# Building the constant mask-edge tile on GpSimd behind the first gate/up blocks

## The chip, the cores and the metric

The kernel runs on one core of a Trainium2 chip. The metric is the device time of one execution in microseconds. A core has five engines that run side by side, each through its own in-order stream of instructions: TensorE (PE, matmuls; its weight loads are shown as PEld), VectorE (DVE), ScalarE (ACT), GpSimd (POOL) and SyncE (SP, which issues most of the DMAs here). They wait for one another by semaphores.

## What is computed

One normalised input goes through two branches whose sums are added to it: a causal sliding-window attention (32 heads of 20, window 256) and a gated MLP.

```python
xn = layernorm(x)                         # x: 1 x 2048 x 640, bf16
q, k, v = split(xn @ wqkv)                # 32 heads of 20
scores = q @ k.T * 20 ** -0.5
mask = (i - j >= 0) & (i - j < 256)       # query i, key j
o = softmax(where(mask, scores, -1e9)) @ v
A = o @ wo
h = sigmoid(xn @ w_gate) * (xn @ w_up)    # 2048 x 1536
B = h @ w_down
return x + A + B
```

## The kernel before, in words

The 2048 rows are worked in four chunks of 512 (c = 0 to 3). For each chunk the kernel normalises x, projects q, k and v, runs the gate and up projections in twelve blocks of 128 hidden units, computes scores and p times v, and at the end multiplies with w_down and wo and adds x.

Scores are made in steps. A step of the function scores fills one PSUM tile ps with scores of four heads for two groups, laid in units of 64 keys by 64 queries (matmuls at L487); ScalarE takes the exponential into a bf16 tile pT (L493); then the units that the mask cuts through are trimmed. In most steps GpSimd does this with four affine selects (L504): two of 64 x 512 elements for the diagonal units of either half of the partitions, and two of 64 x 256 for the oldest units. In steps with the key "late" (one of five per head pair from the second chunk on) the trimming is one VectorE instruction, a minimum with the constant tile edge (L497), which is 128 x 512, zero where the mask forbids and a huge number elsewhere. The steps of the first chunk, the table FIRST, have no "late".

Edge is built by make_edge (L238): one memset (L239) and four affine selects of 64 x 256 (L243), all on GpSimd. It is called at L675, when the code has already emitted the first chunk's norms and projections. GpSimd has no part in those beyond constants and memsets, so in its own stream edge follows directly on the memsets of the v tiles (L320, L321) and precedes the first select.

The function pv (L508) multiplies the pT tiles of one head pair with v (L520). In the first chunk it reads four score tiles in nine pieces; each piece is a set of eight small matmuls, and a matmul waits for those selects of its tile that it reads. The last piece belongs to the fourth tile.

The order of the work from L677 on is written by a small planner. fill is a list of parts, each a generator with a cost in nanoseconds of TensorE. Between the score steps the main loop (L719) pulls matmul work out of the parts in order, as much as a budget allows; the first pull (L715) takes six half gate/up blocks ahead of the first score step. A part made by later() runs its function once, at cost 0, when the parts in front of it are used up. The first part, gu0a, holds gate/up blocks 0 to 3 of the first chunk, with the statistics of the second chunk's norm mixed in between. The reciprocal roots of those norms are two GpSimd instructions (rstds, L266 and L267); from them VectorE makes the normalised rows xn (L272), which SyncE's queue transposes by DMA into xnT (L283). The order of each engine's stream is the order in which this code emits instructions; nothing reorders them afterwards.

Of the kernel before, what the change touches and what calls it, by code (L numbers as in the profile page):

```python
# [93 lines left out]
def kernel(  # L94
# [95 lines left out]
    def load_rest():  # L190
        load_gu(wg, B_w_gate, 1, 0, FS // 2)
        load_gu(wu, B_w_up, 1, 0, FS // 2)
        load_gu(wg, B_w_gate, 1, FS // 2)
        load_gu(wu, B_w_up, 1, FS // 2)
        spread("q", 0, 4, NG)
        spread("k", 0, 4, NG)
# [39 lines left out]
    edge = const.tile([P, HG, 2 * U], BF16, name="edge")  # L236

    def make_edge():  # L238
        nc.gpsimd.memset(edge, BIG)  # L239
        for k, base, sign in ((0, -1, -1), (1, 0, 1)):  # L240
            for a in range(2):
                view = edge[a * U:(a + 1) * U, :, k * U:(k + 1) * U]
                nc.gpsimd.affine_select(out=view, in_=view, pattern=[[0, HG], [sign, U]],  # L243
                                        compare_op=GE, fill=0.0, base=base, channel_multiplier=-sign)
# [98 lines left out]
    def g_norms(c, turn, gap=3):  # L343


        new_xnT(c)
        mvs = lnp.tile([P, SBC, nc.vector.BN_AGGR_DIM], FP32, name="mvs", bufs=1)
        for s in range(SBC):
            ln_block(c, s, mvs[:, s, :])
            if s == SBC - 1:  # L350
                rstds = rstd_blocks(mvs)
            yield 0
        for _ in range(gap):
            yield 0
        for s in range(SBC):
            norm_block(c, s, mvs[:, s, :], rstds[:, s:s + 1])
            yield 0
            if turn:
                turn_block(c, s)
# [43 lines left out]
    def part(w, d, f):  # L403
        k, first = divmod(f * P, FS)
        return w[k][:, d, first:first + P]

    def g_gu(c, f0, f1):
        for f in range(f0, f1):
            pg = ps_d.tile([P, CW], FP32, name="pg", tag="d")
            for d in range(DC):  # L410
                nc.tensor.matmul(pg, lhsT=part(wg, d, f), rhs=xnT[c][:, d, :],  # L411
                                 start=(d == 0), stop=(d == DC - 1))
            th = tp.tile([P, CW], FP32, name="th")
            nc.scalar.activation(out=th, in_=pg, func=TANH, scale=0.5)  # L414
            yield 5 * MM
            pu = ps_d.tile([P, CW], FP32, name="pu", tag="d")
            for d in range(DC):
                nc.tensor.matmul(pu, lhsT=part(wu, d, f), rhs=xnT[c][:, d, :],  # L418
                                 start=(d == 0), stop=(d == DC - 1))
            h = hp.tile([P, CW], BF16, name="h")  # L420
            ht[c, f] = h
            nc.vector.scalar_tensor_tensor(out=h, in0=th, scalar=1.0, in1=pu, op0=ADD, op1=MULT)  # L422
            yield 5 * MM
# [171 lines left out]
    def mix(a, b, first, every=1, rest=True):  # L595

        for k, cost in enumerate(a):
            yield cost
            if k >= first and (k - first) % every == 0:
                yield next(b, 0)  # L600
        if rest:
            yield from b
# [69 lines left out]
    for _ in g_qk(0):  # L672
        pass
    load_rest()
    make_edge()  # L675

    fill = Fill()  # L677
    GU = 10 * MM
# [3 lines left out]
    def later(load, *args):  # L682
        load(*args)
        yield 0
# [2 lines left out]
    norms2 = g_norms(2, True)  # L687
    norms3 = g_norms(3, False, 6)
    fill.add("gu0a", mix(g_gu(0, 0, 4), norms1, 4, 1, False), 4 * GU)
    fill.add("gu0b", mix(g_gu(0, 4, 12), norms1, 0), 8 * GU)  # L690
    fill.add("x2", later(load_x, 2), 0)
    fill.add("wo_i", later(turn_wo), 0)
# [114 lines left out]
```

## Time and profile before

| what | value |
|---|---|
| time, median of three runs | 309.31 us (308.95 to 309.39) |
| span of the profiled execution | 307.5 us |
| granted TensorE clock | 1.000 over the span |
| busy: TensorE, ScalarE, VectorE, GpSimd | 299.6, 198.4, 170.7, 169.3 us |
| edge: memset and four selects on GpSimd | 0.69 us at 3.18, and 1.79 us from 3.94 |
| first mask select on GpSimd (L504) | 32.70 us |
| first use of edge (L497) | 94.2 us |

The profile is of one execution; its span runs from the first to the last instruction. The time of a run is a little longer than the span; the profile gives no time of its own for the profiled execution besides the span, and the three runs' median lies 1.8 us above it. In the rows that follow, a line of the time order has the start, the duration, the engine, the source line, the operation and its tiles, and in brackets the idle time before it with what ended it. Several equal instructions behind one another are merged into one row (x4). The chain of work that ended last is followed back from the last instruction, at each step to what released it.

### The profile page before, as it was taken

Reading aid. Unit: us, or ns where it says so; the run is one execution under the profiler, and the core shown is the slowest. Engines: PE = TensorE matmul, PEld = TensorE weight load, DVE = VectorE, ACT = ScalarE, POOL = GpSimd, SP = SyncE. Lnnn points to the kernel's source line nnn. Section 1 sums busy time; section 2 is a strip of 40 time slices with the busy share of each in tenths; the row PEclk is TensorE's granted clock in tenths of the full one; section 3 lists DMA queues with packets and bytes.
Section 4 is the critical chain, followed back from the end, with each engine's and each line's share of the span. In section 5 each row is a group of like instructions: output and inputs, shape, how many; then the busy total and the mean of one; then the engine's idle time right before and its main releaser. Section 6 shows DMA issues by size and latency. Waiting matters only on the chain.

```text
span 307.5 us, 9944 instructions
## 1 busy us (share of the span) xinstructions
PE 299.6 (97%) x4276; PEld 167.5 (54%) x4311; DVE 170.7 (56%) x339; ACT 198.4 (65%) x197; POOL 169.3 (55%) x308
## 2 busy tenths in 40 slices
PE   7999999999999999999999999999999999999995
PEld 3654444555657654554457654554546664444774
DVE  5633666639698364487946164392824536363523
ACT  6933877698855649888674547878585547687000
POOL 6000686787874828576683729467372937566000
PEclk9999999999999999999999999999999999999999
DMA  7997976986407352820002712730000200000202
GB/s 215 366 344 236 324 158 214 337 238 209 154 2 139 58 179 68 272 83 2 3 3 67 129 58 87 250 122 0 5 0 2 87 26 21 2 2 7 83 21 67
DMA packets 40460, 35.68 MB, mean 116 GB/s; under 512 B 10560, under 2 KB 39872, under 8 KB 40384
## 3 DMA queue, kind: packets, MB, share of 16 engines
q1 hardware_dynamic: 39552, 34.27, 37.3%
q10 hardware_dynamic: 864, 0.77, 0.9%
q8 instruction: 34, 0.56, 0.8%
q14 instruction: 10, 0.08, 0.1%
HBM read 23.63 MB, written 10.26 MB: 110 GB/s over the span
## 4 chain that ended last, share of the span: by engine, by line
PE 96%; issue 1%; DMA 1%; DVE 1%; ACT 0%; SPq 0%
PE y L432 18%; PE pu L418 17%; PE pg L411 17%; PE pqk L297 14%; PE ps L487 9%; PE pv L326 7%; PE y L439 7%; PE acc L520 6%; DMA xc<-in_A_x_dram 1%; PE pt L279 0%; ACT xn L617 0%; DVE xn L272 0%; DVE xn L628 0%; SPq L156 0%; DVE stats L252 0%
## 5 line engine op out<-in xcount | busy, mean ns | idle before, releaser
L504 POOL TENSOR_SCALAR_AFFINE_SELECT pT<-pT 64x512 bf16<-64x512 bf16 (+1 forms) x256 | 157.7, 616 | 108.1 <-ACT pT L493 95.6
L493 ACT ACTIVATE pT<-ps 128x2048 bf16<-128x2048 f32 (+1 forms) x76 | 141.0, 1855 | 59.6 <-PE ps L487 54.6
L422 DVE SCALAR_TENSOR_TENSOR h<-th,pu 128x512 bf16<-128x512 f32 x48 | 32.8, 684 | 52.6 <-PE pu L418 46.1
L418 PE MATMUL pu<-xnT,wu 128*128 128x512 bf16 x228 | 59.0, 380 | 0.7 <-issue 0.2
L411 PE MATMUL pg<-xnT,wg 128*128 128x512 bf16 x226 | 58.5, 380 | 0.9 <-issue 0.3
L432 PE MATMUL y<-wd,h 128*128 128x320 bf16 (+2 forms) x396 | 56.7, 295 | 0.0
L432 PEld LDWEIGHTS <-h 128*128 128x128 bf16 x396 | 36.7, 98 | 15.8 <-issue 2.0
L414 ACT ACTIVATE th<-pg 128x512 f32<-128x512 f32 x48 | 28.6, 595 | 15.5 <-PE pg L411 15.4
L411 PEld LDWEIGHTS <-wg 128*128 128x128 bf16 x240 | 22.2, 98 | 25.8 <-issue 1.8
L418 PEld LDWEIGHTS <-wu 128*128 128x128 bf16 x240 | 22.0, 98 | 25.5 <-issue 2.0
L487 PE MATMUL ps<-qT,kT 20*64 20x320 bf16 (+4 forms) x1440 | 32.1, 260 | 0.0
L532 DVE STREAM_TRANSPOSE t<-acc 128x512 f32<-128x512 f32 x32 | 21.1, 697 | 19.7 <-PE acc L520 19.7
L487 PEld LDWEIGHTS <-kT 20*64 20x64 bf16 x1440 | 15.4, 103 | 24.9 <-issue 21.8
L443 DVE SCALAR_TENSOR_TENSOR rows<-y,rows 128x320 bf16<-128x320 f32 x30 | 14.4, 488 | 25.5 <-PE y L439 25.3
L544 DVE TENSOR_TENSOR on<-t,rec 128x320 bf16<-128x320 f32 (+4 forms) x48 | 27.8, 580 | 1.1
L326 PE MATMUL pv<-wv,xnT 128*128 128x320 bf16 x160 | 25.7, 300 | 0.0
L439 PE MATMUL y<-wo,oc 128*128 128x320 bf16 (+2 forms) x165 | 24.2, 295 | 0.0
L297 PE MATMUL pqk<-xnT,wk 128*128 128x512 bf16 x97 | 23.1, 381 | 0.2
L297 PE MATMUL pqk<-xnT,wq 128*128 128x512 bf16 x94 | 22.8, 381 | 0.4 <-issue 0.2
L335 DVE CAST v<-pv 64x320 bf16<-64x320 f32 x29 | 14.1, 486 | 12.5 <-PE pv L326 12.3
L520 PE MATMUL acc<-pT,v 64*32 64x320 bf16 (+4 forms) x1440 | 19.7, 253 | 0.0
L520 PEld LDWEIGHTS <-v 64*32 64x32 bf16 x1440 | 16.2, 91 | 5.8 <-ACT pT L493 1.7
(50 smaller groups left out, 178.7 us busy)
## 6 DMA issues: line engine op xcount, KB each, us to landing
qT<-sq SPq DMA_DIRECT2D x16, 256.0 KB
kT<-sk SPq DMA_DIRECT2D x16, 256.0 KB
sq<-st SPq DMA_DIRECT2D x20, 128.0 KB
sk<-st SPq DMA_DIRECT2D x20, 128.0 KB
out_dram<-rows SPq DMA_DIRECT2D x15, 160.0 KB
wg<-in_B_w_gate_dram SPq DMA_DIRECT2D x4, 480.0 KB
wu<-in_B_w_up_dram SPq DMA_DIRECT2D x4, 480.0 KB
xc<-in_A_x_dram SPq DMA_DIRECT2D x3, 640.0 KB
```

The source lines that it names most:

```text
L297: nc.tensor.matmul(ps, lhsT=wt[:, m, :], rhs=xnT[c][:, d, :], start=(d == 0), stop=(d == DC - 1))
L326: nc.tensor.matmul(ps[:, 0:HALF], lhsT=xnT[c][:, d, s * P:(s + 1) * P], rhs=wqkv[2][:, d, hf * HALF:(hf + 1) * HALF], start=(d == 0), stop ...
L411: nc.tensor.matmul(pg, lhsT=part(wg, d, f), rhs=xnT[c][:, d, :], start=(d == 0), stop=(d == DC - 1))
L414: nc.scalar.activation(out=th, in_=pg, func=TANH, scale=0.5)
L418: nc.tensor.matmul(pu, lhsT=part(wu, d, f), rhs=xnT[c][:, d, :], start=(d == 0), stop=(d == DC - 1))
L422: nc.vector.scalar_tensor_tensor(out=h, in0=th, scalar=1.0, in1=pu, op0=ADD, op1=MULT)
L432: nc.tensor.matmul(y[:, 0:cut[1] - cut[0]], lhsT=ht[c, f][:, s * P:(s + 1) * P], rhs=wd[:, f, cut[0]:cut[1]], start=(f == 0), stop=False)
L439: nc.tensor.matmul(y[:, 0:cut[1] - cut[0]], lhsT=oc[c, m][:, s * P:(s + 1) * P], rhs=wo[:, m, cut[0]:cut[1]], start=False, stop=(m == DC - 1))
L487: nc.tensor.matmul(ps[a * U:(a + 1) * U, i, col * U:(col + n) * U], lhsT=qk["k", kc, o // GH][32 * i:32 * i + DH, o % GH + a, kb * U:(kb + ...
L493: nc.scalar.activation(out=pt[:, :, 0:width], in_=ps[:, :, 0:width], func=EXP, scale=SCALE)
L504: nc.gpsimd.affine_select(out=view, in_=view, pattern=[[0, HG], [0, n], [sign, U]], compare_op=GE, fill=0.0, base=base, channel_multiplier ...
L520: nc.tensor.matmul(acc[32 * i:32 * i + 32, q * U:(q + n) * U], lhsT=vt[kb][a * U:(a + 1) * U, u, h * VW:h * VW + 32], rhs=pt[a * U:(a + 1) ...
```

## The change

make_edge is no longer called in front of the planner. It becomes a part of its own, of cost 0, behind gu0a and in front of gu0b, the gate/up blocks 4 to 11.

```diff
     load_rest()
-    make_edge()
 
     fill = Fill()
...
     fill.add("gu0a", mix(g_gu(0, 0, 4), norms1, 4, 1, False), 4 * GU)
+    fill.add("edge", later(make_edge), 0)
     fill.add("gu0b", mix(g_gu(0, 4, 12), norms1, 0), 8 * GU)
```

The function that is moved stays as it was:

```python
    def make_edge():
        nc.gpsimd.memset(edge, BIG)
        for k, base, sign in ((0, -1, -1), (1, 0, 1)):
            for a in range(2):
                view = edge[a * U:(a + 1) * U, :, k * U:(k + 1) * U]
                nc.gpsimd.affine_select(out=view, in_=view, pattern=[[0, HG], [sign, U]],
                                        compare_op=GE, fill=0.0, base=base, channel_multiplier=-sign)
```

The order in which the instructions are emitted for TensorE, VectorE, ScalarE and SyncE is the same in both kernels. On GpSimd the five instructions of edge move from behind the v memsets to behind the first rstds pair, in front of the selects of the second score tile.

## The prediction

> **What bounds the kernel now.** I read the page's busy table first, then the chain of work that ended last, then the waits of TensorE, and last the time order of GpSimd (POOL) from 0 to 60 us with the other engines around 44 us, where GpSimd first meets TensorE (PE).
>
> ```profile
> PE 299.6 (97%) x4276; PEld 167.5 (54%) x4311; DVE 170.7 (56%) x339; ACT 198.4 (65%) x197; POOL 169.3 (55%) x308
> PE 96%; issue 1%; DMA 1%; DVE 1%; ACT 0%; SPq 0%
> ```
>
> PE is busy for 97% of the span and is 96% of the chain. From 12 us on, the longest single idle time in front of PE or its weight loads is 0.42 us, and nearly all of these have exactly that length, whoever is named: it is what PE pays to change between the 128-row matmuls and the small tiles of the scores (L487) and of p times v (L520). So nothing later in the kernel waits long enough to give a lost PE microsecond back: what PE loses once is added to the end. The question is only whether the moved work makes PE wait.
>
> ```profile
> 3.18 0.69 POOL L239 MEMSET edge<- 128x512 bf16 x1
> 3.94 1.79 POOL L243 TENSOR_SCALAR_AFFINE_SELECT edge<-edge 64x256 bf16<-64x256 bf16 x4
> 32.70 2.40 POOL L504 TENSOR_SCALAR_AFFINE_SELECT pT<-pT 64x512 bf16<-64x512 bf16 x4 [26.96 <-ACT pT L493]
> 35.19 0.23 POOL L266 TENSOR_SCALAR rstds<-mvs 128x4 f32<-128x4 f32 x1
> 35.50 1.04 POOL L267 TENSOR_TENSOR rstds<-rstds,neghalf 128x4 f32<-128x4 f32 x1
> 36.52 10.19 POOL L504 TENSOR_SCALAR_AFFINE_SELECT pT<-pT 64x512 bf16<-64x512 bf16 x16
> 47.90 5.03 POOL L504 TENSOR_SCALAR_AFFINE_SELECT pT<-pT 64x512 bf16<-64x512 bf16 x8 [1.19 <-ACT pT L493]
> ```
>
> This is GpSimd in time order: start, duration, instruction. Today edge is built by 5.73 us, in front of a 26.96 us hole. From 32.70 the hole is over: after the first score tile and the two rstds instructions, sixteen mask selects (four score tiles of four) run back to back until 46.71, and only then does GpSimd wait for ScalarE again, for 1.19 us.
>
> ```profile
> 43.48 0.69 DVE L422 SCALAR_TENSOR_TENSOR h<-th,pu 128x512 bf16<-128x512 f32 x1 [0.86 <-PE pu L418]
> 44.38 0.82 PEld L520 LDWEIGHTS <-v 64*32 64x32 bf16 x72 [0.42 <-POOL pT L504]
> 44.38 1.04 PE L520 MATMUL acc<-pT,v 64*32 64x320 bf16 x72
> 45.35 0.29 PEld L487 LDWEIGHTS <-kT 20*64 20x64 bf16 x24
> 45.96 1.88 ACT L493 ACTIVATE pT<-ps 128x2048 bf16<-128x2048 f32 x1 [0.87 <-PE ps L487]
> ```
>
> The first p-times-v group starts at 44.38 and reads score tiles 1 to 4. Windows of a few hundredths of a microsecond give the last select of tile 4 at 43.74 to 44.20, and the last of the group's nine pieces (the five-unit piece of tile 4) at 45.08, its second half of the partitions at about 45.10. With 0.06 us from a finished producer to PE (the first xn on VectorE ends at 5.45, its transpose on PE starts at 5.51), GpSimd is ahead of PE here by 45.10 - 44.20 - 0.06 = 0.84 us. That margin is the whole cover of the change.
>
> **The change, part by part.** *Where the five instructions go.* On PE, ScalarE, VectorE and the SyncE queue the order stays as it was, and make_edge issues no DMA. On GpSimd the memset and four selects leave the place behind the v memsets and come directly behind the second rstds instruction and in front of the selects of score tile 2.
>
> *What the removal gives at the start.* 2.5 us of GpSimd, which nobody there waits for: the next GpSimd work starts 27 us later. One neighbour is touched: VectorE's first xn (L272) took 0.64 us at 4.81 beside the edge selects, and the same instruction 0.45 us at 7.61 beside an idle GpSimd. Freed, it ends 0.19 earlier. But the next reciprocal on the chain (5.77) also needs ScalarE's root, which ends at 5.72 and is heard 0.04 later, at 5.76. So 0.01 of the 0.19 can reach PE, with 0.19 as the far end if that root were not in the way; I take 0.
>
> *What the insertion costs on GpSimd.* Memset: its row says 0.69, but it was issued while the memset before it still ran, until 3.44, and ended at 3.87, which leaves 0.43. The memsets of 128 and 1536 columns (0.205 and 1.38 us) put 512 columns at 0.53; I take that, with 0.43 and 0.69 as ends. Then 0.07 to the first select, 1.79 for four, and 0.07 to the next instruction: 2.46 (2.36 to 2.62). There is no hole to absorb it: the rstds end at 36.54 and tile 2's exponential ends at 36.43.
>
> *How late tile 4 is.* Tile 2 starts at 36.52 + 2.46 = 38.98. Tiles 2 to 4 took 7.68 us (36.52 to 44.20), with 0.07 of waiting for tile 4's exponential (41.61), which is long done now. Two of their six long selects met an xn on VectorE and took 0.75 instead of 0.67; the xn still start at 38.85 and 41.47 and meet two selects again, of tiles 2 and 3. So tile 4 ends at 38.98 + 7.61 = 46.59, 2.39 late.
>
> *What PE pays.* The first five pieces run as before. Piece six needs the first selects of tile 4 (about 44.8 and 45.5 now) and waits some tenths; the last piece needs the fourth, heard at 46.65. PE therefore leaves this group 46.65 - 45.10 = 1.55 us late, and everything behind it in its in-order stream is late by that. For the ends: the edge block 0.10 less or 0.16 more, and the meetings with VectorE another 0.1 either way, give 1.35 to 1.8.
>
> *Who is late next.* Behind the group stand the scores of tile 6 and its exponential, today 45.96 to 47.84 and then 47.84 + 1.55 = 49.39. GpSimd, through with tile 5 at about 49.05, is idle again before that. The 1.19 hole plus PE's own delay swallow the lateness, so PE waits only once. rstds stays ahead of edge, so the xn and their transposing DMAs for the second chunk are on time. Edge itself is first read at 94.2 us (L497), 55 us after it is ready.
>
> *A rule against the rows.* The pairs 0.75 against 0.67 and 0.64 against 0.45 are what GpSimd and VectorE cost each other here. The Trainium skill, page "SBUF — State Buffer", section "Who interferes with whom", says that such a VectorE instruction and a GpSimd instruction share one port pair, and that whichever starts second blocks until the first has ended. By that rule the start shows a wait on VectorE's side, which the 0.64 agrees with, but a select that comes second would lose a whole xn, 0.41 to 0.45, instead of 0.08. If the moved order made one more select lose that, the stall would be near 2.0 us and the time 311.3; the rows before show no such loss, and I keep 0.08.
>
> *Sum.* The profiled execution has a span of 307.5; the median of the runs is 309.31, so about 1.8 lies around the span and I leave it alone. 307.5 + 1.55 - 0.0 = 309.05 span, 309.31 + 1.55 = 310.9 in time, 0.5% more.
>
> **The rivals.** *One wait for the whole group.* If PE's first matmul of the group waited for all four tiles, PE would start it at 46.65 instead of 44.38: +2.27, 311.6. For it: the row at 44.38 names POOL. Against it: the 0.42 there is the usual change of tile, and the instruction list has ten separate waits on GpSimd inside the group, one for each tile and half at its first use, which one early wait would make needless. Chance 0.08.
>
> *Not slower: the block hides.* The v memsets start every 0.05 us and last 0.2 to 0.39, so GpSimd's records do overlap. Were the edge block to cost it less than the 0.84 of margin, PE would not wait: 309.3. It decides at a lateness of 0.84 for no change at all, and 1.46 for a change too small to see. Against it: the four edge selects stand 0.45 apart and last 0.41, so they do not overlap, and they alone are 1.79. Chance 0.05.
>
> *The lateness stays.* If GpSimd did not catch up before the next p-times-v group (56.9 us), PE would wait there again, at most as long: up to 312.4. Against it: the holes of 1.19, 1.18 and 0.18 us in front of its selects between 47 and 57 us. Chance 0.04.
>
> **How the numbers follow.** The forecast, one stall of 1.55 at the first group, has 0.80; its own range is 310.5 to 311.2 (1.35 to 1.8, with 0.1 for the scatter of a median). The three rivals hold 0.17; 0.03 is for the unforeseen, 0.02 of it faster, 0.01 same. About 0.2% (0.6 us) is what can be told from no change. Slower: 0.80 + 0.08 + 0.04 = 0.92. Same: 0.05 + 0.01 = 0.06. Faster: 0.02. The range reaches up to the first rival and down by the smallest stall with some scatter: 310.3 to 311.6.
>
> **What would show it.** Right: edge's memset at about 36.5, tile 2's selects from about 39.0, a gap of over 1 us inside the first L520 group with POOL pT L504 named, the next scores 1.5 us later, no second such wait, and GpSimd's first wait for ScalarE again near 49. The first xn would last about 0.45, with the first v projection where it was. Wrong: L520 unbroken from 44.38 (the margin was larger or the block shorter), the group starting as a whole near 46.6 (one wait), or a PE gap that shrinks later (something did give time back).

## The result, and the profile after

The changed kernel takes 310.8 us (median of 12, 310.51 to 311.45) where the kernel before takes 309.13 in the same comparison: a ratio of 1.005, 95% interval 1.0038 to 1.0063. Run again on another occasion it took 310.73 against 309.20, a ratio of 1.0054 (1.0037 to 1.0071). It is slower by about 1.6 us, as forecast (310.9). Two of the kernels below (two selects the first time, and twice at the start) had their profile taken in an execution of 1273 and of 507 us, far from their medians; from these two profiles only the closing wait is used.

The profiled execution has a span of 309.3 us. First the busy table and the head of the chain of the page, after:

```profile
PE 300.3 (97%) x4276; PEld 167.9 (54%) x4311; DVE 170.6 (55%) x339; ACT 198.5 (64%) x197; POOL 169.4 (55%) x308
PE 94%; DMA 2%; issue 1%; ACT 1%; POOL 1%; SPq 1%; DVE 0%
```

Busy times are as they were. What is new and matters is GpSimd's 1% in the chain; ScalarE's 1% and the higher share of the DMAs are explained below, by a false link and a late load. GpSimd's time order shows the five instructions in their new place:

```profile
33.13 2.40 POOL L504 TENSOR_SCALAR_AFFINE_SELECT pT<-pT 64x512 bf16<-64x512 bf16 x4 [29.70 <-ACT pT L493]
35.62 0.23 POOL L266 TENSOR_SCALAR rstds<-mvs 128x4 f32<-128x4 f32 x1
35.94 1.04 POOL L267 TENSOR_TENSOR rstds<-rstds,neghalf 128x4 f32<-128x4 f32 x1
36.94 0.53 POOL L239 MEMSET edge<- 128x512 bf16 x1
37.54 1.80 POOL L243 TENSOR_SCALAR_AFFINE_SELECT edge<-edge 64x256 bf16<-64x256 bf16 x4
39.40 10.17 POOL L504 TENSOR_SCALAR_AFFINE_SELECT pT<-pT 64x512 bf16<-64x512 bf16 x16
49.95 5.03 POOL L504 TENSOR_SCALAR_AFFINE_SELECT pT<-pT 64x512 bf16<-64x512 bf16 x8 [0.38 <-ACT pT L493]
```

From the memset's start to the first select of tile 2 it is 39.40 - 36.94 = 2.46 us. By 49.57 the sixteen selects (score tiles 2 to 5) are through, and GpSimd waits again, 0.38 us, for the next exponential: it no longer holds anybody up. The first p-times-v group in TensorE's time order, with its weight loads and the next scores:

```profile
44.81 0.66 PEld L520 LDWEIGHTS <-v 64*32 64x32 bf16 x45 [0.42 <-POOL pT L504]
44.82 0.82 PE L520 MATMUL acc<-pT,v 64*32 64x320 bf16 x44
46.11 0.83 PE L520 MATMUL acc<-pT,v 64*32 64x192 bf16 x24 [0.47 <-POOL pT L504]
47.15 0.32 PE L520 MATMUL acc<-pT,v 64*32 64x320 bf16 x4 [0.21 <-POOL pT L504]
47.40 0.29 PEld L487 LDWEIGHTS <-kT 20*64 20x64 bf16 x24
```

The group starts at once. The rows show two breaks: behind 44 matmuls, when the second half of tile 4's diagonal is missing, and behind 24 more, when the last half of its oldest unit is. Narrower windows show two more inside the merged rows: PE starts again at 45.38, 46.11, 46.63 and 47.15, each time 0.04 to 0.06 us behind the end of one of tile 4's four selects (45.33, 46.06, 46.57 and 47.11). From the group's start to the next scores it is 47.40 - 44.81 = 2.59 us, where it was 45.35 - 44.38 = 0.97: PE loses 1.62. The two idle times that the rows name add up to 0.68 only, because a merged row also holds the pauses between its own matmuls; the loss is read from start to start.

The chain in order of time runs through the same place:

```profile
42.80 1.88 ACT pT L493
44.68 0.65 POOL pT L504
45.32 0.07 issue
45.39 0.67 POOL pT L504
46.05 0.07 issue
46.12 0.45 POOL pT L504
46.57 0.07 issue
46.64 0.47 POOL pT L504
47.11 0.04 issue
47.15 0.32 PE acc L520 x4
```

The four GpSimd steps are tile 4's selects, and the last of them releases PE at 47.15. One link is misleading: the chain lets ScalarE's exponential of 42.80 to 44.68 release the first of them. That is tile 5's exponential, which ended there by chance; tile 4's had ended at 40.18 + 1.87 = 42.05. What held tile 4 was GpSimd's own queue, in which the selects run back to back from 39.40 on, behind edge. A releaser is inferred from what ended last, and here it hides the cause.

At the start one row moved. The first xn on VectorE, after, and the same in the kernel that builds edge at both places (add_only, below):

```profile
4.86 0.45 DVE L272 TENSOR_SCALAR xn<-xc,mv,rstd 128x640 bf16<-128x640 bf16 x1
```

```profile
4.83 0.63 DVE L272 TENSOR_SCALAR xn<-xc,mv,rstd 128x640 bf16<-128x640 bf16 x1
```

It is 0.18 us shorter without edge's selects beside it, and nothing comes of that: the next root's reciprocal starts at 5.79 in the one and 5.78 in the other. In this profile the group starts 0.44 later than before (44.82 against 44.38), because a load of wv landed late near 8.8 us. In the repeat of the same kernel that offset is 0.16.

### The profile page after: what moved, and what is told of

Read it like the earlier page. It is cut to its first block, busy times and chain, and to the rows that moved or that the text cites. A ratio compares the mean times of both kernels' runs of the same rounds, so it can differ in the third digit from the quotient of the medians.

```text
span 309.3 us, 9944 instructions
## 1 busy us (share of the span) xinstructions
PE 300.3 (97%) x4276; PEld 167.9 (54%) x4311; DVE 170.6 (55%) x339; ACT 198.5 (64%) x197; POOL 169.4 (55%) x308
## 4 chain that ended last, share of the span: by engine, by line
PE 94%; DMA 2%; issue 1%; ACT 1%; POOL 1%; SPq 1%; DVE 0%
PE y L432 17%; PE pu L418 17%; PE pg L411 17%; PE pqk L297 14%; PE ps L487 9%; PE y L439 7%; PE pv L326 7%; PE acc L520 6%; DMA wv<-in_A_wqkv_dram 2%; POOL pT L504 1%; ACT pT L493 1%; SPq L156 1%; SPq L160 0%; ACT th L414 0%; DVE xn L443 0%
## 5 line engine op out<-in xcount | busy, mean ns | idle before, releaser
L504 POOL TENSOR_SCALAR_AFFINE_SELECT pT<-pT 64x512 bf16<-64x512 bf16 (+1 forms) x256 | 157.7, 616 | 109.9 <-ACT pT L493 97.5
L520 PE MATMUL acc<-pT,v 64*32 64x320 bf16 (+4 forms) x1440 | 20.5, 253 | 0.8 <-POOL pT L504 0.7
L520 PEld LDWEIGHTS <-v 64*32 64x32 bf16 x1440 | 16.5, 91 | 7.1 <-issue 1.9
```

The source lines that it names most:

```text
L520: nc.tensor.matmul(acc[32 * i:32 * i + 32, q * U:(q + n) * U], lhsT=vt[kb][a * U:(a + 1) * U, u, h * VW:h * VW + 32], rhs=pt[a * U:(a + 1) ...
```

## The experiments

Each edit is shown against the kernel before, unless something else is said. The theory: what is inserted makes score tile 4 late, 0.84 us of that are covered, and PE loses the rest once. The rivals: the loss comes from the removal at the start; it goes in proportion to the inserted time; any place among the selects costs it.

**Add only.** Edge stays where it was and is built again at the new place.

```diff
     load_rest()
     make_edge()
...
+    fill.add("edge", later(make_edge), 0)
     fill.add("gu0b", mix(g_gu(0, 4, 12), norms1, 0), 8 * GU)
```

> Edge is built at its old place and a second time at the new one, so nothing is removed and only the insertion is tested. Margin theory (the five inserted instructions make score tile 4 late by 2.46 us, of which 0.84 is covered): the whole loss, 309.1 + 1.65 = 310.8, with the breaks in the first p-times-v group as in the changed kernel, and the first xn back at 0.64 us. Rival, part of the loss comes from the removal (the changed kernel's profile has its first chunk 0.43 us late behind a load of wv): 310.3 to 310.4, since nothing is removed here.

310.5 us, ratio 1.0037 (1.0012 to 1.0062). PE's time order in this kernel:

```profile
44.40 0.82 PE L520 MATMUL acc<-pT,v 64*32 64x320 bf16 x44
45.69 0.83 PE L520 MATMUL acc<-pT,v 64*32 64x192 bf16 x24 [0.47 <-POOL pT L504]
46.73 0.32 PE L520 MATMUL acc<-pT,v 64*32 64x320 bf16 x4 [0.21 <-POOL pT L504]
46.98 0.43 PE L487 MATMUL ps<-qT,kT 20*64 20x320 bf16 x24
```

The same breaks, and 2.58 us from group to scores: the whole stall is there with nothing removed. The time, though, fell between the two expectations, nearer to the rival's 310.3 to 310.4. So the change itself and this kernel were run side by side.

**The change again, and add only again.**

> The changed kernel once more, on the chip of the next one. If the removal at the start costs something by itself, this is slower than building edge at both places by about 0.3 (310.8 against 310.5); if not, the two are equal.

> Edge at both places once more, beside the changed kernel. Equal to it (both 310.6 to 310.9) if only the insertion matters; 0.3 faster if the removal costs by itself.

310.73 us for the change (1.0054, 1.0037 to 1.0071) and 310.34 for add only (1.0028, 1.001 to 1.0047). The stall is the same in both: 44.54 to 47.11 and 44.45 to 47.02, 2.57 us each. In time they differ by 0.39, which is what the expectation named for a cost of the removal. The last VectorE instruction starts at 305.73 and at 305.58, against 303.97 before, so the work itself is 1.76 and 1.61 later. The rest of the difference lies behind the work: the spans, 309.0 and 308.4, are 0.6 apart. The SyncE queue's wait for the last store is 1.5 in both; its closing wait for TensorE's queue is not, first the change, then add only (the time of all such waits, how many, the longest):

```profile
SPq L802 <- PEq L802: 1.0, 2, 0.9
```

```profile
SPq L803 <- PEq L803: 0.6, 2, 0.4
```

The barrier that closes the program waits 1.0 us in one and 0.6 in the other. It is 1.0 in all profiles of kernels with 308 instructions on GpSimd, and 0.6 in all of those with 313, in which edge is built twice. Whether five more instructions alone shorten the time was tried:

**Twice at the start.** The kernel before with make_edge called twice at its old place, and not at the new one.

```diff
     load_rest()
     make_edge()
+    make_edge()
```

> The kernel before with edge built twice over at its old place and nothing at the new one: five more GpSimd instructions in a stretch where GpSimd idles for 27 us. Building edge at both places was 0.39 us faster than the change itself, although PE waited equally long (2.33 us from the start of the first p-times-v group to its last piece, in both); in its profile the closing barrier is 0.4 to 0.5 shorter (a wait of 0.6 instead of 1.0 behind the last store). If that comes with the five more instructions, this one is 0.4 us faster than before, 308.8, with the same 0.6. If it comes from edge being built early, or from chance, it is 309.2 with 1.0.

309.01 us against 309.06, ratio 0.999 (0.9972 to 1.0007). The barrier shows 0.6 in its profile (the one of 507 us), but the time is not 0.4 shorter: the fastest run is 0.27 below the fastest of before, the medians 0.05. So the shorter barrier goes with the five more instructions, and what it is worth stays open, and with it the cause of the 0.39 between the change and add only. The rival of a cost of the removal rests on this difference alone, and the next experiment speaks against it.

**The hole.** Edge is built not at all at the start, but behind the first p-times-v group (against the changed kernel).

```diff
-    fill.add("edge", later(make_edge), 0)
...
             pv(*pair, parts.pop(pair))
+            if pair == (0, 0):
+                make_edge()
```

> Edge is built behind the first p-times-v group, which on GpSimd is between the selects of score tiles 5 and 6, in front of its two holes of 1.2 us each. Same instructions, same busy stretch, one pair of groups later. Margin theory: tile 6 starts 1.3 us late, tile 8 ends 0.1 to 0.2 late, within the second group's margin, and PE does not wait: 309.1. Rival, any place among the selects costs about the same: 310.3 or more. Rival, part of the loss comes from the removal at the start: 309.5.

309.12 us, ratio 0.9995 (0.9977 to 1.0012): no difference from before. GpSimd and PE in time order:

```profile
36.53 10.19 POOL L504 TENSOR_SCALAR_AFFINE_SELECT pT<-pT 64x512 bf16<-64x512 bf16 x16
46.78 0.53 POOL L239 MEMSET edge<- 128x512 bf16 x1
47.37 2.04 POOL L243 TENSOR_SCALAR_AFFINE_SELECT edge<-edge 64x256 bf16<-64x256 bf16 x4
49.48 9.87 POOL L504 TENSOR_SCALAR_AFFINE_SELECT pT<-pT 64x512 bf16<-64x512 bf16 x16
60.43 5.88 POOL L504 TENSOR_SCALAR_AFFINE_SELECT pT<-pT 64x512 bf16<-64x512 bf16 x9 [1.09 <-ACT pT L493]
```

```profile
44.39 1.04 PE L520 MATMUL acc<-pT,v 64*32 64x320 bf16 x72
56.89 1.06 PE L520 MATMUL acc<-pT,v 64*32 64x320 bf16 x72
```

The same five instructions, again in front of sixteen selects back to back, cost 2.7 us of GpSimd and nothing else. The holes that were there before, of 1.19, 1.18 and 0.18 us, took up nearly all of it, so the sixteen selects end at 59.35, where the same ones ended at 59.14 before, and the second group (56.89, before 56.88) runs through. The removal at the start is in this kernel too, and costs nothing that shows. So it is neither the removal nor the busy stretch; it is the place ahead of the one group with 0.84 us of margin.

**Two selects, three selects, edge twice.** The inserted time is varied. In the first two the memset and the remaining selects stay at the start (here for three; two keeps two); the last builds edge twice at the new place. Both edits are against the changed kernel.

```diff
-    def make_edge():
-        nc.gpsimd.memset(edge, BIG)
+    def make_edge(which=(0, 1, 2, 3)):
+        if 0 in which:
+            nc.gpsimd.memset(edge, BIG)
...
+                if 2 * k + a not in which:
+                    continue
...
+    make_edge((0,))
...
-    fill.add("edge", later(make_edge), 0)
+    fill.add("edge", later(make_edge, (1, 2, 3)), 0)
```

```diff
-    fill.add("edge", later(make_edge), 0)
+    fill.add("edge", later(lambda: (make_edge(), make_edge())), 0)
```

> The memset and two of edge's four selects stay at the start, the other two are at the new place: some 0.94 us inserted instead of 2.46. Margin theory: tile 4 late by 0.94, 0.84 covered, so PE loses 0.1 to 0.2: 309.2 to 309.3, not to be told from before. Rival, every inserted microsecond costs PE its share (1.67 for 2.46): 0.64 more, 309.8.

> The kernel with two of edge's selects at the new place once more, for a profile. Margin theory, corrected by the kernel with three (1.4 us inserted, PE lost 0.34): with 0.95 inserted PE loses nothing, the first p-times-v group runs without a break, 309.2.

> The memset and one of edge's four selects stay at the start, three are at the new place: some 1.4 us inserted. Margin theory: tile 4 late by 1.4, 0.84 covered, PE loses 0.55: 309.25 + 0.55 = 309.8, and the last piece of the first p-times-v group breaks off for that long. Rival, in proportion to the inserted time (1.6 for 2.46): 310.15. Rival, the cost sets in as a whole (as soon as the group breaks, 1.5): 310.7.

> Edge is built twice over at the new place and not at the start: 4.92 us inserted. Margin theory: tile 4 late by 4.92, 0.84 covered, PE loses 4.1: 313.2, with the second p-times-v group still unbroken. Rival, cost in proportion to the inserted time: 2 x 1.67, 312.5. Rival, the lateness also reaches the second group: over 314.

Two selects: 309.15 us (1.0001, 0.9988 to 1.0015), the second time 309.19 (1.0001, 0.9982 to 1.002). Three: 309.53 against 309.20 (1.0004, 0.9991 to 1.0018), which by time alone can't be told from no change. Twice: 315.39 (1.0186, 1.0164 to 1.0208), 2.2 us more than expected. GpSimd and PE in time order, with two, with three (in these two kernels L246, L507 and L523 are L243, L504 and L520), and with edge twice:

```profile
36.51 0.90 POOL L246 TENSOR_SCALAR_AFFINE_SELECT edge<-edge 64x256 bf16<-64x256 bf16 x2
37.47 9.86 POOL L507 TENSOR_SCALAR_AFFINE_SELECT pT<-pT 64x512 bf16<-64x512 bf16 x16
44.37 1.04 PE L523 MATMUL acc<-pT,v 64*32 64x320 bf16 x72
45.34 0.43 PE L490 MATMUL ps<-qT,kT 20*64 20x320 bf16 x24
```

```profile
36.75 1.34 POOL L246 TENSOR_SCALAR_AFFINE_SELECT edge<-edge 64x256 bf16<-64x256 bf16 x3
38.16 9.85 POOL L507 TENSOR_SCALAR_AFFINE_SELECT pT<-pT 64x512 bf16<-64x512 bf16 x16
44.53 1.38 PE L523 MATMUL acc<-pT,v 64*32 64x320 bf16 x72
45.84 0.43 PE L490 MATMUL ps<-qT,kT 20*64 20x320 bf16 x24
```

```profile
37.04 0.53 POOL L239 MEMSET edge<- 128x512 bf16 x1
41.95 9.85 POOL L504 TENSOR_SCALAR_AFFINE_SELECT pT<-pT 64x512 bf16<-64x512 bf16 x16
44.92 0.63 PE L520 MATMUL acc<-pT,v 64*32 64x320 bf16 x40
47.61 0.26 PE L520 MATMUL acc<-pT,v 64*32 64x192 bf16 x4 [2.06 <-POOL pT L504]
49.77 0.47 PEld L487 LDWEIGHTS <-kT 20*64 20x64 bf16 x24 [0.28 <-issue]
```

From the group's start to the next scores, less the 0.97 that it takes undisturbed:

| at the new place | GpSimd time inserted | PE loses |
|---|---|---|
| two selects | 37.47 - 36.51 = 0.96 | 0.00 |
| three selects | 38.16 - 36.75 = 1.41 | 0.34 |
| the change | 39.40 - 36.94 = 2.46 | 1.62 (1.60 to 1.61 in its repeat and in add only, twice) |
| edge twice | 41.95 - 37.04 = 4.91 | 3.88 |

Nothing is lost below a threshold, and above it the loss is one for one (1.41 to 4.91 is 3.50 more inserted, 3.54 more lost). A cost in proportion, 0.66 for each, would give 0.63, 0.93, 1.62 and 3.2. The threshold, inserted less lost, reads 1.07 from the row of three and 0.84 from the change. That gap goes with VectorE: the sixteen selects took 9.85 or 9.86 us in the other three rows, but 10.17 in the change, where each pair of xn begins ahead of a long select. The stall of edge twice agrees with the theory (4.1 expected, 3.88; with the threshold of 1.07 it would be 3.84); its time doesn't. The clock does the rest, by the windows of this kernel (start and end, length, busy time of the engines, granted clock, DMA):

```profile
40.00:48.80 8.80, 6.20 (x115) 2.81 (x101) 3.49 (x6) 5.12 (x5) 7.92 (x16) 1.00 0.80 131
48.80:55.60 6.80, 6.45 (x58) 2.28 (x59) 4.03 (x9) 2.63 (x3) 5.12 (x10) 0.50 0.60 213
55.60:62.00 6.40, 6.24 (x58) 2.69 (x58) 1.80 (x4) 4.33 (x5) 2.94 (x6) 1.00 0.93 342
```

From 48.8 on, while the group still waits for its last piece, the granted clock is 0.50 for 6.8 us. PE's gate block that starts at 49.36 before starts at 56.48 here, 7.1 later, of which 0.5 were there at the group's start and 3.9 are the loss of the table; the remaining 2.7 came in this stretch. The single runs agree: the mean granted clock was 0.989 in the three runs of 315.39 to 315.62 us, 0.993 in the one of 315.03 and 0.995 in the one of 313.88, and 6.8 us at half clock would make it 0.989. That this is the clock, and follows from PE standing still, was tested by keeping PE busy.

**Edge twice, with PE busy.** Twelve 128 x 512 matmuls on constants, whose result nobody reads, run ahead of the first group, on top of the edit of edge twice.

```diff
             fill.hurry = pair[1] == NG - 2
+            if pair == (0, 0):
+                warm = ps_d.tile([P, CW], FP32, name="pwarm", tag="d")
+                for n in range(12):
+                    nc.tensor.matmul(warm, lhsT=ones[:, 0:P], rhs=ones, start=(n == 0), stop=(n == 11))
```

> As the kernel that builds edge twice over at the new place, with twelve extra 128 x 512 matmuls on constants (2.6 us, their result unused) ahead of the first p-times-v group, which still waits for the same selects. In the doubled kernel PE stood nearly still from 45.6 to 48.3 us, and the granted clock was 0.50 from about 48.8 to 55.6. Clock theory: the wait alone costs 3.8, the halved clock 2.8 more; with PE kept busy through most of the wait the clock stays at 1.00 and the time is 309.25 + 3.8 to 4.1 = 313.0 to 313.4 although PE has more to do. Rival, the 2.8 have another cause (lateness of the engines behind, which the extra work doesn't change): 315.4 or more.

313.75 us, ratio 1.0142 (1.0104 to 1.0181), against the 315.39 of edge twice alone, which has less work on PE. The two intervals overlap a little, so the profile and the clocks of the single runs have to decide. The same windows and the group:

```profile
40.00:48.80 8.80, 8.58 (x115) 3.88 (x115) 3.19 (x5) 4.84 (x5) 7.92 (x16) 1.00 0.73 155
48.80:55.60 6.80, 6.54 (x72) 2.82 (x69) 5.34 (x10) 4.41 (x4) 5.88 (x11) 1.00 0.68 233
```

```profile
44.55 2.79 PE L731 MATMUL pwarm<-const-bfloat16-1.0 128*128 128x512 bf16 x12
47.27 1.61 PE L520 MATMUL acc<-pT,v 64*32 64x320 bf16 x68
49.33 0.43 PE L487 MATMUL ps<-qT,kT 20*64 20x320 bf16 x24
```

The wait for tile 4 ends where it must (next scores 4.78 behind 44.55, so 3.81 lost), and the clock stays at 1.00. The extra 2.7 are gone in this profile (its span is 311.3). The median is above the 313.0 to 313.4 expected: the four runs at a clock of 0.999 or more took 312.58 to 313.77, all less than any of edge twice, and the other two, at 0.995, took 316.12 and 318.37. What slowed those two is open.

No version beat the kernel before: with edge in its old place, or in the hole, its GpSimd time is hidden altogether.

## Why the prediction was right

- **The insertion**: 2.46 us forecast (2.36 to 2.62), 2.46 measured; the memset's own cost, taken as 0.53 between 0.43 and 0.69, is 0.53 in the row.
- **Tile 4**: 7.61 us for tiles 2 to 4 forecast, 39.40 to 47.11 = 7.71 measured. The two selects that meet an xn took 0.84 and 0.79. The forecast took both at 0.75, but one of them was at 0.79 before already (that of 39.03). This term was mis-sized by 0.1, inside the 0.1 that the bounds gave it. No select lost a whole xn, so the 311.3 that the forecast set beside its sum did not come.
- **The margin and the stall**: 0.84 and 1.55 forecast; 1.60 to 1.62 measured in four profiles; tile 4's 0.1 covers the difference. The row of three selects lost 0.34 where 0.55 was expected: there the selects meet no xn that began before them, so tile 4 comes 0.2 earlier.
- **The start**: the first xn went from 0.64 to 0.45 and reached nobody, as forecast. A wait for wv that the forecast did not have set this profile's group back by 0.44; with edge gone from the start the offset ranges from 0.01 to 0.54 over five profiles, with edge there it is 0.02 and 0.07. Whether the removal has a part in that is open; the hole kernel, with the removal, is not slower than before.
- **Once only**: GpSimd waits again from 49.57, and the second group is unbroken. The rival of a lasting lateness fell here, and in the hole kernel.
- **The rivals**: one wait for the whole group fell with the 44 matmuls that ran from 44.82, and with the four restarts. (The ten waits that the forecast counts in the instruction list are in no trace; four of them show as these restarts.) The hidden block fell with edge's five rows, end to end.
- **The signs to look for**: "a gap of over 1 us" was the wrong picture. The loss is spread over several short breaks, in PE's rows at most 0.47 long.
- **A reading that was too strong**: that nearly all idle times in front of PE have the length of 0.42. Over half of those before its weight loads from 12 us on last 0.20 to 0.27. None is longer than 0.42, and that is all that the argument needs: what PE lost at the first group, 1.60 of the repeat's 1.76, was still lost at the end.

The time came out at 310.8, 0.1 below the 310.9 forecast and 1.67 above before, for a stall of 1.62. That it fits so closely is partly luck. In the repeat the work ends 1.76 later, with 0.16 of start offset that the forecast took at 0, and the time is only 1.53 longer, because less lies behind the last VectorE instruction's start (309.0 - 305.73 = 3.27, where it was 307.5 - 303.97 = 3.53). These two nearly cancel.

## What to carry to other kernels

Before moving work on an engine that "has time", find the next place where the bounding engine reads that engine's output, and take the margin there: 138 us of GpSimd idle over the span (307.5 less 169.3 busy) did not help, 0.84 us decided. Beyond the margin GpSimd's lateness reached PE one for one, and in front of holes it cost nothing, so the same five instructions four score tiles further on are free. Read a stall from start to start across the group, and distrust a releaser whose end merely coincides.

## What the runs showed of the hardware

TensorE's granted clock fell to 0.50 although PE never stood idle for more than 2.06 us. In the kernel with edge twice, between 45.55 and 48.34 us only four small matmuls ran; the clock is 1.00 until 48.7, 0.50 from 48.8 to 55.6, and 1.00 again, and that cost 2.7 us more than the wait. The stall of the change itself, 1.6 us broken into pieces, left it at 1.00. The Trainium skill, page "TensorE: Matmul & The Clock Gate", part 1, states that the clock halves after about one idle window of 3.4 us and that the window runs freely. The trace agrees in the halving and in the order of time (3.2 us from the first gap to the fall); it also shows that a few matmuls inside do not prevent it.

Selects on GpSimd and the xn on VectorE slow each other, and mostly the one that begins second is slowed. A 64 x 512 select takes 0.66 us when it began first (the kernel with three selects, at 38.88; its xn, from 38.99, then took 0.73), and 0.84 when an xn of 0.44 was under way (the change, xn from 39.28, select from 39.40). The kernel with two selects has an exception: an xn from 38.84 took 0.72, although a 64 x 512 select was just ending then (38.86) and the one beside it, 64 x 256, began only at 38.92 and took its usual 0.45. The first two pairs fit the rule of the Trainium skill that the prediction draws on (page "SBUF — State Buffer", section "Who interferes with whom") in its order. In size they don't show it: the select of the change lost 0.18 us, while that xn had 0.32 left.
